# Four unread transposes of the identity on PE at the end of each step of the first batch

## The chip, the cores and the metric

One Trainium2 chip, of which the program uses one core. The metric is the device time of one execution in microseconds (us), lower is better. Five engines work side by side, each on its own list of instructions in the order written: PE (matrix products and transposes), DVE (VectorE), ACT (ScalarE), POOL (GpSimd) and SP, which issues most DMA transfers.

## The reference, cut to what matters

Sliding-window attention with sink keys on 4 batches of 8 heads (768 positions, head size 64), then a gated MLP with a convolution of three taps over the positions:

```
scores = scale * q @ k.T                       # per batch and head
keep   = key < n_sink or 0 <= row - key < window      # n_sink 4, window 128
a      = exp(scores - max) / (sum + 1e-9)      # where keep, else 0
x      = a @ v                                 # heads side by side: 768 x 512 per batch
h      = relu(x @ w_in)                        # 768 x 1024
conv   = conv_w[0]*h[s-1] + conv_w[1]*h[s] + conv_w[2]*h[s+1]
out    = (h * sigmoid(conv)) @ w_out           # 768 x 512 per batch
```

## The kernel before, in words

The heads go in pairs, g = 0 to 15, four pairs to a batch. A pair has six tiles of 128 query rows, t = 0 to 5. One tile of one pair is one step of the loop at line 630. The first batch has 24 steps (NSTB); they run over the first halves of its four pairs and then over the second halves. The other batches run pair by pair.

In step i the loop records, in three slots:

- scores(g, t), line 488: two products on PE, one per head (j = 0, 1), into two PSUM tiles of the tag sc. There are two buffers of this tag, so that j = 0 always has the one and j = 1 the other. Then DVE masks the scores (L508) and reduces them to the row's extreme (L509), ACT takes the exponential with its sum (L512), DVE the reciprocal (L514, L515), POOL the product (L517). In the first batch the products are plain (L339, 260 columns; 128 for t = 0); later each is a sum of two (L342, L343).
- transp of the step before (line 526): two transposes of the probabilities on PE (L532), a copy on ACT (L534), two selections on POOL (L536, L538); at the third tile of a half also the sink columns (L546).
- pv of two steps before (line 558): at the third tile of a half the products with the values (L573, L576) into px, which ACT and DVE store as the MLP's input (L350, L351).

Between the slots stand pieces of other work. The MLP of a part of a batch that is ready is cut into pieces (first products L183, gate L190 to L201, second products L210), spread evenly by a rate over the next steps. For the first batch the first part becomes ready after half of its steps, the second after all of them. The turns of q and k of coming pairs (L318; L276 and L294 from the second batch on) come at due times. In steps 2 to 18 the weights are converted, one piece per step (WHEN, line 35): they are read as 64-bit numbers, narrowed on DVE (L112, L113, L114) and split on ACT and POOL or DVE (L121, L122).

The recorded order isn't the order on the engines. When the program is built, a scheduler puts each engine's instructions in an order of its own, from a model of their times, and adds the waits that the tiles need: a PSUM or SBUF tile may only be written anew when its readers are done. So a change of a few instructions can move all that comes after them. For the waits a tile is one thing: whoever writes one part of it also waits for those who read another.

Of the kernel before, what the change touches and what calls it, by code (L numbers as in the profile page):

```python
# [10 lines left out]
F32 = mybir.dt.float32  # L11
# [6 lines left out]
P = 128  # L18
# [6 lines left out]
SW = 2 * P + NS  # L25
# [6 lines left out]
TRAIL = 2  # L32
NGB = TRAIL + 2
LA = 1
WHEN = list(range(2, 19))


# [23 lines left out]
class Moe:  # L61
# [92 lines left out]
    def need(self, n):  # L154

        while self.done < n:
            self.fetch(self.done + 1)
            self.todo[self.done][2](self.raws[self.done])
            self.done += 1
            self.fetch(self.done + LA)  # L160

# [222 lines left out]
def sink_split(c, m, vsr, b):  # L384

    raw, hi, lo = (m.mp.tile([P, 512], d, tag="st", name=f"sink{n}{b}", bufs=3)[0:NS] for d, n in ((F32, "r"), (F32R, "h"), (F32R, "l")))
    c.nc.sync.dma_start(raw.rearrange("s (h d) -> s h d", d=D), c.v[b].rearrange("h s d -> s h d")[0:NS])
    c.nc.scalar.copy(hi, raw)
    c.nc.vector.tensor_tensor(out=lo, in0=raw, in1=f(hi), op=ALU.subtract)
    for u in range(3):  # L390
        for part, val in enumerate((hi, hi, lo)):
            for j in range(2):
                r = SR * part + 2 * NS * u + NS * j
                dst, src = (f(x).rearrange("s (g j d) -> s g j d", j=2, d=D)[:, :, j] for x in (vsr[r:r + NS, u], val))
                c.nc.sync.dma_start(dst, src)


def banded(c):

    nc = c.nc  # L400
    m = Moe(c)
    A = Attn(c, m.x, KW, m.mp, m.ps)
# [4 lines left out]
    ap, ps = A.ap, A.ps  # L407
# [37 lines left out]
    def clear():  # L445
        w = vsr.shape[1] * vsr.shape[2] // 2
        for h in range(2):
            nc.sync.dma_start(f(vsr).rearrange("p u n -> p (u n)")[:, w * h:w * h + w], A.zeros[0:3 * SR, 0:w])
# [29 lines left out]
    def fetch(upto=len(queue)):  # L478

        while free[0] and asked[0] < min(len(queue), upto):  # L480
            free[0] -= 1
            g, nm, half = queue[asked[0]]
            st[g].raw[nm, half] = load_half(c, g, nm, half, c.raw[asked[0] % RAWB])
            asked[0] += 1
# [3 lines left out]
    def scores(g, t):  # L488
        s = st[g]
        lo = 0 if t == 0 else (t - 1) * KW  # L490
        mk = m0 if t == 0 else (m1 if t == 1 else m2)
        cols = slice(NS if t == 0 else 0, KW)
        sm = sms[A.tiles % len(sms)]
        A.tiles += 1
        hf, u = divmod(t, 3)
        if u == 0:
            s.pe[hf] = ap.tile([P, 3, 2, KW], F32, tag="pe", name=f"pe{g}_{hf}")
            if t == 0:
                nc.gpsimd.memset(s.pe[hf][:, 0, :, 0:NS], 0.0)
        pe = s.pe[hf][:, u]  # L500
        pcs = [ps.tile([P, SW], F32, tag="sc", name=f"sc{g}_{t}_{j}", bufs=2) for j in range(2)]
        if t == 0:
            A.scores(s, t, [pc[:, KW:SW] for pc in pcs], lo, lo + P)
        else:
            A.scores(s, t, pcs, lo, lo + SW)
        for j, pc in enumerate(pcs):
            if t:
                nc.vector.copy_predicated(pc[:, KW:SW], before.bitcast(I32), pc[:, 0:P])  # L508
            nc.vector.tensor_tensor_reduce(out=pe[:, j, cols], in0=pc[:, P:SW][:, cols], in1=mk, op0=ALU.add, op1=ALU.min,  # L509
                                           scale=1.0, scalar=3.0e38, accum_out=sm[:, j:j + 1])  # L510
        for j in range(2):
            nc.scalar.activation(pe[:, j, cols], pe[:, j, cols], AF.Exp, bias=sm[:, j:j + 1], scale=-1.0,  # L512
                                 accum_out=sm[:, 2 + 2 * j:3 + 2 * j])
        nc.vector.tensor_reduce(out=sm[:, 6:8], in_=sm[:, 2:6].rearrange("p (j e) -> p j e", e=2), op=ALU.add, axis=mybir.AxisListType.X)  # L514
        nc.vector.reciprocal(sm[:, 8:10], sm[:, 6:8])  # L515
        for j in range(2):
            nc.gpsimd.tensor_scalar(pe[:, j, cols], pe[:, j, cols], sm[:, 8 + j:9 + j], 1.0, ALU.mult, ALU.mult)  # L517
# [40 lines left out]
    def pv(g, t):  # L558

        s = st[g]  # L560
        hp = g % NPAIR
        hf, u = divmod(t, 3)
        if u < 2:
            return
        px = ps.tile([P, 3, P], F32, tag="px", name=f"px{g}_{hf}").rearrange("p t k -> p (t k)")
        first = 3 * hf
        tiles = range(first + 2, max(0, first - 1) - 1, -1)
        for kt in tiles:
            pT = s.pT.pop((kt, hf)).rearrange("p h a k -> p h (a k)")
            lo, hi = max(kt, first), min(kt + 1, first + 2)  # L570
            cols = slice(P * (lo - kt), P * (hi - kt) + P)
            for j in range(2):
                nc.tensor.matmul(px[D * j:D * j + D, P * (lo - first):P * (hi - first) + P], s.v[:, kt, j, :], pT[:, j, cols],  # L573
                                 start=(kt == tiles[0]), stop=False, skip_group_check=True)
        for w in range(1 - hf, 3):
            nc.tensor.matmul(px[:, P * w:P * w + P], (vsr if g >= NPAIR else c.vs)[:, w, P * hp:P * hp + P], s.sT, start=False, stop=(w == 2),  # L576
                             skip_group_check=True)
        A.xout(g, hf, px)
# [3 lines left out]
    def prep(n):  # L582

        g, half = jobs[n]
        if g >= NPAIR and half:
            return []
        if g >= PLAIN:
            return A.prep(g, st[g], ahead)
        if half == 0 and g % 2 == 0:
            kks.append(f(ap.tile([P, 4, T, KW], F32R, tag="kk", name=f"kk{g}")))  # L590
        out = []
        for h in (half, half + 1)[0:1 + g // NPAIR]:
            out += A.prep32(g, h, st[g], kks[g // 2][:, g % 2], "po" if g < NPAIR and h == 0 else "h", ahead)
        return out

    def values(n):
        g, half = jobs[n]
        if g < NPAIR:
            st[g].v = load_v(c, g, n % 2, *((2, T) if half else (0, 3)))
        elif half == 0:  # L600
            st[g].v = load_v(c, g, g % 2)

    def coming(n):

        last = 2 * NPAIR - 2
        if n < last:
            return [(n + 1, -0.4, 1.8)]
        if n == last:
            return [(n + 1, -0.4, 1.4), (n + 2, 1.4, 5.6)]
        return [(n + 2, -0.4, 5.1)] if n % 2 == 0 and n + 2 < len(jobs) else []  # L610
# [10 lines left out]
    NSTB = NPAIR * T  # L621
# [8 lines left out]
    for i in range(NST + D2):  # L630
        if i < NST:
            n, g, t = steps[i]
            if t % 3 == 0:
                for n1, lo, hi in coming(n):
                    new = prep(n1)
                    todo += [(i + lo + (hi - lo) * (k + 1) / len(new), x) for k, x in enumerate(new)]
            if g >= NPAIR or t % 3 == 2:
                fetch()
            if t == 0 and g and g % NPAIR == 0:
                after = i + 3 if g > NPAIR else i  # L640
            if i == after:
                sink_split(c, m, vsr, g // NPAIR)
            if n + 1 < len(jobs) and (t % 3 == 2 if n < 2 * NPAIR else t == 3):
                values(n + 1)
        if i == NSTB // 2:
            clear()
        m.need(min(sum(i >= w for w in WHEN), len(m.todo)))
        for slot in range(SLOTS):
            if slot == 0 and i < NST:
                scores(g, t)  # L650
            if slot == 1 and 0 <= i - D1 < NST:
                transp(*steps[i - D1][1:])
            if slot == 2 and 0 <= i - D2 < NST:
                pv(*steps[i - D2][1:])
                if i - D2 + 1 in cuts:
                    while fill:
                        fill.pop(0)()
                    lo, hi, span = cuts[i - D2 + 1]
                    fill = m.pieces(lo, hi)
                    rate = len(fill) / (span - 0.5)  # L660
                    acc = 0.0
            acc += rate / SLOTS
            while acc >= 1.0 and fill:
                fill.pop(0)()
                acc -= 1.0
            while todo and i + (slot + 1) / SLOTS >= todo[0][0]:
                todo.pop(0)[1]()
    while fill:
        fill.pop(0)()

# [70 lines left out]
def attention_gated_mlp(ctx: ExitStack, tc: tile.TileContext, q, k, v, n_sink, window, w_in, conv_w, w_out, out):  # L741
# [33 lines left out]
    with tc.If(fast == 1) as cmp:  # L775
        with ExitStack() as es:
            c.es = es
            banded(c)
# [32 lines left out]
```

## Time and profile before

| what | us |
|---|---|
| median of three runs | 489.8 |
| lowest and highest of them | 489.42, 490.3 |
| the profiled execution's own time | 490.03 |
| its span, from the first to the last instruction | 488.3 |
| PE busy | 457.4 (94% of the span) |
| DVE busy | 348.4 (71%) |
| ACT busy | 340.5 (70%) |
| POOL busy | 312.7 (64%) |
| mean granted clock of PE | 0.983 of full speed |

The span begins with the first instruction on the core; 1.73 us of the profiled execution's own time lie outside of it. A busy time holds an instruction from its start to its end. PE's matrix instructions overlap, so that a busy PE isn't one at its peak. The trace shows a product of 32-bit numbers as two instructions and a transpose of 128 columns as one. The granted clock is the share of full speed that PE was given in a stretch.

### The profile page before, as it was taken

Reading aid. Unit: us, or ns where it says so; the run is one execution under the profiler, and the core shown is the slowest. Engines: PE = TensorE matmul, PEld = TensorE weight load, DVE = VectorE, ACT = ScalarE, POOL = GpSimd, SP = SyncE. Lnnn points to the kernel's source line nnn. Section 1 sums busy time; section 2 is a strip of 40 time slices with the busy share of each in tenths; the row PEclk is TensorE's granted clock in tenths of the full one; section 3 lists DMA queues with packets and bytes.
Section 4 is the critical chain, followed back from the end, with each engine's and each line's share of the span. In section 5 each row is a group of like instructions: output and inputs, shape, how many; then the busy total and the mean of one; then the engine's idle time right before and its main releaser. Section 6 shows DMA issues by size and latency. Waiting matters only on the chain.

```text
span 488.3 us, 10470 instructions
## 1 busy us (share of the span) xinstructions
PE 457.4 (94%) x3149; PEld 389.7 (80%) x3149; DVE 348.4 (71%) x1212; ACT 340.5 (70%) x1086; POOL 312.7 (64%) x614
## 2 busy tenths in 40 slices
PE   2887798899999999999999999999999999999995
PEld 2555477688889888888888888888888888999993
DVE  4798989957968777786677585886675665656553
ACT  3887858778878977786877786876776754545451
POOL 3584796867976867684758577685764564344441
PEclk9988989999999999999999999999999999999998
DMA  5778653537234132334132332324021100101011
GB/s 147 211 229 212 172 168 79 126 85 188 67 72 116 61 83 66 87 96 99 60 77 58 85 81 60 70 63 98 24 55 33 44 3 0 44 2 44 1 44 53
DMA packets 87307, 41.03 MB, mean 84 GB/s; under 512 B 80160, under 2 KB 80184, under 8 KB 87240
## 3 DMA queue, kind: packets, MB, share of 16 engines
q1 hardware_dynamic: 87096, 39.99, 31.5%
q8 instruction: 28, 0.46, 0.4%
q14 instruction: 39, 0.32, 0.2%
q10 hardware_dynamic: 144, 0.26, 0.2%
HBM read 27.60 MB, written 6.29 MB: 69 GB/s over the span
## 4 chain that ended last, share of the span: by engine, by line
PE 80%; DVE 7%; DMA 3%; issue 3%; ACT 2%; POOL 2%; SPq 1%; DVEq 0%; ACTq 0%; POOLq 0%
PE po L210 27%; PE ph L183 26%; PE px L573 8%; PE sc L342 4%; PE pts L532 4%; PE sc L343 3%; PE px L576 2%; PE tq L276 2%; PE tk L294 2%; PE sc L339 2%; POOL pe L517 1%; DVE sc L508 1%; DMA wi_1r<-in_moe_w_in_dram 1%; DVE pe L509 1%; DVE stm L113 1%
## 5 line engine op out<-in xcount | busy, mean ns | idle before, releaser
L210 PE MATMUL po<-woH,g 128*128 128x512 f32 x384 | 142.0, 409 | 1.2 <-POOL g L200 1.0
L183 PE MATMUL ph<-xH,wiH 128*128 128x258 f32 (+1 forms) x384 | 112.2, 292 | 1.2 <-ACT X L255 1.2
L183 PE MATMUL ph<-xH,wiL 128*128 128x258 f32 (+1 forms) x384 | 109.0, 284 | 0.0
L183 PE MATMUL ph<-xL,wiH 128*128 128x258 f32 (+1 forms) x384 | 108.8, 284 | 0.0
L517 POOL TENSOR_SCALAR pe<-pe,sm 128x132 f32<-128x132 f32 (+1 forms) x192 | 82.8, 442 | 34.9 <-DVE sm L515 27.2
L512 ACT ACTIVATE pe<-pe,sm 128x132 f32<-128x132 f32 (+1 forms) x192 | 77.5, 406 | 15.8 <-DVE sm L509 14.7
L200 POOL TENSOR_SCALAR g<-t 128x256 fp32r<-128x256 f32 x96 | 42.2, 439 | 70.7 <-DVE t L198 50.8
L195 DVE SCALAR_TENSOR_TENSOR t<-hb,cw,t 128x256 f32<-128x256 f32 x96 | 54.0, 562 | 36.6 <-ACT t L194 36.1
L201 POOL TENSOR_TENSOR g<-t,g 128x256 fp32r<-128x256 f32 x96 | 75.2, 784 | 5.6
L210 PEld LDWEIGHTS po<-woH,g 128*128 128x128 f32 x384 | 68.7, 189 | 11.6 <-POOL g L200 2.6
L183 PEld LDWEIGHTS ph<-xH,wiH 128*128 128x128 f32 x384 | 73.0, 190 | 5.5 <-ACT X L255 1.6
L210 PE MATMUL po<-woL,g 128*128 128x512 f32 x192 | 76.4, 398 | 0.0
L183 PEld LDWEIGHTS ph<-xH,wiL 128*128 128x128 f32 x384 | 72.9, 190 | 2.1
L183 PEld LDWEIGHTS ph<-xL,wiH 128*128 128x128 f32 x384 | 72.8, 190 | 0.7
L197 ACT ACTIVATE t<-t 128x256 f32<-128x256 f32 x96 | 40.1, 418 | 33.8 <-DVE t L196 33.4
L198 DVE SCALAR_TENSOR_TENSOR t<-t,hb 128x256 f32<-128x256 f32 x96 | 47.5, 494 | 20.1 <-ACT t L197 19.0
L508 DVE COPY_PREDICATED sc<-before,sc 128x128 f32<-128x128 int32 x160 | 45.6, 291 | 22.6 <-PE sc L343 19.1
L509 DVE CUSTOM_DVE_ANT_0 pe<-sc,m 128x132 f32<-128x132 f32 (+1 forms) x192 | 54.0, 288 | 10.3 <-PE sc L343 7.8
L190 ACT ACTIVATE hb<-ph 128x258 f32<-128x258 f32 (+1 forms) x96 | 37.0, 386 | 31.4 <-PE ph L183 30.7
L536 POOL TENSOR_SCALAR_AFFINE_SELECT pT<-pT 128x256 f32<-128x256 f32 x80 | 38.2, 477 | 31.4 <-ACT pT L534 31.1
L196 DVE SCALAR_TENSOR_TENSOR t<-hb,cw,t 128x256 f32<-128x256 f32 x96 | 54.1, 564 | 4.1
L194 ACT ACTIVATE t<-hb,cw 128x256 f32<-128x256 f32 x96 | 49.2, 513 | 7.7 <-POOL g L201 3.9
(124 smaller groups left out, 930.2 us busy)
## 6 DMA issues: line engine op xcount, KB each, us to landing
raw<-in_q_dram SPq DMA_DIRECT2D x64, 96.0 KB
raw<-in_k_dram SPq DMA_DIRECT2D x64, 96.0 KB
out_dram<-stm SPq DMA_DIRECT2D x23, 256.0 KB
kk<-kk SPq DMA_DIRECT2D x24, 198.0 KB
vraw<-in_v_dram SPq DMA_DIRECT2D x24, 192.0 KB
wi_0r<-in_moe_w_in_dram SPq DMA_DIRECT2D x2, 512.0 KB
wi_1r<-in_moe_w_in_dram SPq DMA_DIRECT2D x2, 512.0 KB
wi_2r<-in_moe_w_in_dram SPq DMA_DIRECT2D x2, 512.0 KB
```

The lines of the kernel that those rows point to most:

```text
L183: nc.tensor.matmul(u.h[:, 0:W], w[:, cc, ff * P:(ff + 1) * P], x[:, cc, t0:t1], start=(i == 0), stop=(i == len(prods) - 1))
L194: nc.scalar.mul(a, prev, cw[:, 0, ff:ff + 1])
L195: nc.vector.scalar_tensor_tensor(out=e, in0=this, scalar=cw[:, 1, ff:ff + 1], in1=a, op0=ALU.mult, op1=ALU.add)
L196: nc.vector.scalar_tensor_tensor(out=a, in0=nxt, scalar=cw[:, 2, ff:ff + 1], in1=e, op0=ALU.mult, op1=ALU.add)
L198: nc.vector.scalar_tensor_tensor(out=a, in0=e, scalar=1.0, in1=this, op0=ALU.add, op1=ALU.mult)
L200: nc.gpsimd.tensor_scalar(u.g[:, 0], a, 1.0, 1.0, ALU.mult, ALU.mult)
L201: nc.gpsimd.tensor_tensor(out=u.g[:, 1], in0=a, in1=f(u.g[:, 0]), op=ALU.subtract)
L210: nc.tensor.matmul(po[:, 0:c.DM], u.g[:, a, tt * P:(tt + 1) * P], w[:, ff, :], start=(ff == 0 and i == 0), stop=(ff == NFF - 1 and i == 2))
L508: nc.vector.copy_predicated(pc[:, KW:SW], before.bitcast(I32), pc[:, 0:P])
L509: nc.vector.tensor_tensor_reduce(out=pe[:, j, cols], in0=pc[:, P:SW][:, cols], in1=mk, op0=ALU.add, op1=ALU.min, scale=1.0, scalar=3.0e38, ...
L512: nc.scalar.activation(pe[:, j, cols], pe[:, j, cols], AF.Exp, bias=sm[:, j:j + 1], scale=-1.0, accum_out=sm[:, 2 + 2 * j:3 + 2 * j])
L517: nc.gpsimd.tensor_scalar(pe[:, j, cols], pe[:, j, cols], sm[:, 8 + j:9 + j], 1.0, ALU.mult, ALU.mult)
```

## The change

The two score tiles of a step are now whole PSUM banks of 512 columns, of which the scores use the first 260, as before. Columns 384 to 511 of the second one (j = 1) are kept as A.spare. At the end of each of the first 24 steps PE makes four transposes of the 128 x 128 identity into them. Nobody reads what they write. Nothing else is changed: the count of buffers, the work of the other engines and the DMA transfers are the same.

```
+IDLE = 4
...
-        pcs = [ps.tile([P, SW], F32, tag="sc", name=f"sc{g}_{t}_{j}", bufs=2) for j in range(2)]
+        pcs = [ps.tile([P, 512], F32, tag="sc", name=f"sc{g}_{t}_{j}", bufs=2) for j in range(2)]
+        A.spare = pcs[1][:, 384:384 + P]
+        pcs = [pc[:, 0:SW] for pc in pcs]
...
             while todo and i + (slot + 1) / SLOTS >= todo[0][0]:
                 todo.pop(0)[1]()
+        if i < NSTB:
+            for k in range(IDLE):
+                nc.tensor.transpose(A.spare, c.ident, c.ident)
```

The scheduler gives all engines a new order. The 96 transposes stand in 24 groups, most of them whole. Three places on PE show what happens. In the names below, sc_3_0 is the tile of step t = 3 and j = 0, ph and po are the MLP's first and second products, trq and trk turns of q and k, pts the transposed probabilities; what an instruction waits for stands in brackets by engine (Activation is ACT, DMAHW a transfer). Lines of the kernel after are 1 to 6 higher than before: L339 is now L340, L532 is L535, and the new transposes are L673.

The first place is PE at the second and third product pair of the kernel. Before:

```order
L318 MATMUL trq_220<-ident,raw_69 128x128 x2
L339 MATMUL sc_1_0_227<-kk_174,X_179 128x260 [waits DVE_49,Activation_49]
L339 MATMUL sc_1_1_228<-kk_174,X_179 128x260 [waits DVE_49]
L318 MATMUL trk_245<-ident,raw_70 128x128 [waits DMAHW4_49,DMAHW3_49,PE_49]
L318 MATMUL trk_245<-ident,raw_70 128x128 x2
L532 MATMUL pts<-ident,pe_0_206 128x128 [waits Pool_49]
L339 MATMUL sc_2_0_265<-kk_174,X_179 128x260 [waits DVE_49,PE_49]
```

The same place on PE after:

```order
L340 MATMUL sc_1_0_231<-kk_174,X_179 128x260 [waits DVE_49,Activation_49]
L673 MATMUL sc_0_1_209<-ident 128x128 [waits DVE_49]
L673 MATMUL sc_0_1_209<-ident 128x128 x3
L319 MATMUL trk_249<-ident,raw_70 128x128 [waits DMAHW4_49,DMAHW3_49,PE_49]
L319 MATMUL trk_249<-ident,raw_70 128x128 x2
L535 MATMUL pts<-ident,pe_0_206 128x128 [waits Pool_49]
L340 MATMUL sc_1_1_232<-kk_174,X_179 128x260 [waits DVE_49,PE_49]
L340 MATMUL sc_2_0_273<-kk_174,X_179 128x260 [waits PE_49]
```

The group of the first step waits for DVE, which reads the same tile; the second product of the second step, sc_1_1, now comes behind the group, a turn and a transpose.

The second place is PE in the second half of the first batch, about 55 us into the span before, where the first MLP pieces begin. Before:

```order
L532 MATMUL pts<-ident,pe_1_670 128x128 [waits Pool_49]
L339 MATMUL sc_3_0_827<-kk_174,X_701 128x260 [waits DVE_49,PE_49]
L339 MATMUL sc_3_1_828<-kk_174,X_701 128x260 [waits DVE_49,PE_49]
L339 MATMUL sc_4_0_894<-kk_174,X_701 128x260 [waits DVE_49,PE_49]
L339 MATMUL sc_4_1_895<-kk_174,X_701 128x260 [waits DVE_49,PE_49]
L339 MATMUL sc_5_0_973<-kk_174,X_701 128x260 [waits DVE_49,PE_49]
L532 MATMUL pts<-ident,pe_1_670 128x128 [waits Activation_49,Pool_49]
L532 MATMUL pts<-ident,pe_1_670 128x128 [waits Pool_49]
L210 MATMUL po_948<-woH,g_808 128x512 [waits Pool_49]
```

The same place on PE after:

```order
L184 MATMUL ph_867<-xL_117,wiH 128x258
L673 MATMUL sc_5_1_829<-ident 128x128 [waits DVE_49]
L673 MATMUL sc_5_1_829<-ident 128x128 x3
L340 MATMUL sc_3_1_888<-kk_174,X_749 128x260 [waits DVE_49,PE_49]
L340 MATMUL sc_4_0_958<-kk_174,X_749 128x260 [waits PE_49]
L535 MATMUL pts<-ident,pe_1_718 128x128 [waits Activation_49,Pool_49]
L535 MATMUL pts<-ident,pe_1_718 128x128 [waits Pool_49]
L673 MATMUL sc_3_1_888<-ident 128x128 [waits DVE_49]
L673 MATMUL sc_3_1_888<-ident 128x128 x3
L340 MATMUL sc_4_1_959<-kk_174,X_749 128x260 [waits DVE_49,PE_49]
L549 MATMUL tk_5_911<-ident,sk_1_912 96x128 [waits Activation_49]
L184 MATMUL ph_932<-xH_116,wiH 128x258
```

Where five products with scores stood in a row, each behind a wait for DVE, they now stand apart, with the groups, two transposes and an MLP unit among them.

The third place is PE at the first scores of the second batch, about 100 us into the span before. Before (tq is a turn of q in the second batch):

```order
L532 MATMUL pts<-ident,pe_1_1192 128x128 [waits Pool_49] x2
L276 MATMUL tq_1272<-identr,nq_1241 128x128 [waits Activation_49]
L276 MATMUL tq_1272<-identr,nq_1241 128x128 x2
L342 MATMUL sc_0_0_1398<-kk_1156,X_1244 128x128 [waits DMAHW1_49,DVE_49,PE_49]
L343 MATMUL sc_0_0_1398<-kk_1156,X_1244 128x128
L210 MATMUL po_948<-woH,g_1235 128x512 [waits Pool_49]
```

The same place on PE after:

```order
L673 MATMUL sc_4_1_1342<-ident 128x128 [waits DVE_49]
L673 MATMUL sc_4_1_1342<-ident 128x128 x3
L340 MATMUL sc_5_1_1429<-kk_297,X_1135 128x260 [waits DVE_49,PE_49]
L277 MATMUL tq_1454<-identr,nq_1405 128x128 [waits Activation_49]
L277 MATMUL tq_1454<-identr,nq_1405 128x128 x2
L535 MATMUL pts<-ident,pe_1_1276 128x128 [waits Pool_49] x2
L343 MATMUL sc_0_0_1494<-kk_1236,X_1328 128x128 [waits DMAHW4_49,PE_49]
```

The last but one of the groups stands right ahead of the first batch's last score product, which in turn is close to the second batch's first; the last group comes 18 rows behind the latter.

## The prediction

> **What bounds the kernel now.** I read the page first, its span and the slices of PE and of PE's clock.
>
> ```profile
> span 488.3 us, 10470 instructions
> PE   2887798899999999999999999999999999999995
> PEclk9988989999999999999999999999999999999998
> ```
>
> A slice is 12.2 us. From the ninth on (98 us) PE is full at full clock, to the end. Before that it has gaps, and the clock is lower in places. So the end is PE's work plus what it loses in the first 100 us, which is also where the change puts its transposes. I cut these 100 us by a table of busy times (per row: stretch, its length, PE, PEld, DVE, ACT, POOL, each with its count, then PE's clock).
>
> ```profile
> 7.66:28.14 20.48, 16.37 (x83) 11.78 (x82) 16.46 (x79) 17.20 (x60) 11.97 (x28) 1.00 0.83 221
> 28.14:41.79 13.65, 9.32 (x51) 6.15 (x49) 12.86 (x46) 11.62 (x39) 12.42 (x23) 0.87 0.75 214
> 41.79:48.61 6.82, 6.74 (x40) 5.24 (x41) 5.03 (x14) 3.99 (x11) 1.36 (x4) 0.75 0.87 240
> 48.61:65.68 17.07, 12.91 (x66) 9.38 (x65) 16.64 (x56) 12.99 (x43) 13.98 (x20) 0.80 0.55 156
> 65.68:69.09 3.41, 3.41 (x22) 2.99 (x22) 1.62 (x5) 2.45 (x8) 3.41 (x5) 1.00 0.46 154
> 69.09:96.40 27.31, 23.37 (x154) 18.10 (x153) 26.54 (x78) 20.64 (x61) 20.77 (x32) 1.00 0.53 128
> 96.40:106.64 10.24, 10.24 (x78) 8.83 (x79) 5.22 (x23) 7.66 (x29) 7.79 (x19) 1.00 0.20 45
> ```
>
> The reader sees stages with different limits. From 28.14 to 41.79, 48.61 to 65.68 and 69.09 to 96.40 us DVE is busy 94%, 97% and 97% of the time, and PE has 4.33, 4.16 and 3.94 us of gaps: there DVE sets the pace. From 41.79 to 48.61 PE is full, at a clock of 0.75, and DVE has gaps. From 96.40 on PE is full at full clock and DVE half idle: there each added PE instruction is paid for. In the first stretch nobody is full; it is a chain over all engines.
>
> Then the clock. It changes only on a grid of 3.41 us (the same table, PE alone, cut at that grid).
>
> ```profile
> 14.49:17.90 3.41, 2.25 (x14) 1.00 0.64 146
> 28.14:31.55 3.41, 1.63 (x10) 1.00 0.92 258
> 31.55:34.96 3.41, 3.33 (x11) 0.50 0.85 276
> 38.38:41.79 3.41, 0.93 (x7) 1.00 1.11 265
> 41.79:45.20 3.41, 3.33 (x16) 0.50 0.98 261
> 55.44:58.85 3.41, 1.47 (x6) 1.00 0.60 190
> 58.85:62.27 3.42, 1.84 (x4) 0.50 0.00 1
> 62.27:65.68 3.41, 3.41 (x13) 0.50 0.53 154
> 72.51:75.92 3.41, 1.82 (x14) 1.00 0.97 236
> ```
>
> Three windows in which PE was busy 1.63, 0.93 and 1.47 us are followed by one at half clock; those with 1.82 and 2.25 us are not. The line runs between 1.63 and 1.82 us of 3.41. Four windows ran at half clock.
>
> **The change part by part.** The wider PSUM tile costs nothing: the products write the same 260 columns, the count of buffers is the same, and no other engine gets an instruction. What is added is 96 transposes. Their price is the spacing in a row of like instructions, at full clock and at half:
>
> ```profile
> 92.72 0.27 PE L532 MATMUL pts<-ident,pe 128*128 128x128 f32 x1
> 78.18 0.49 PE L318 MATMUL trq<-ident,raw 128*128 128x128 f32 x3
> 14.36 0.33 PE L532 MATMUL pts<-ident,pe 128*128 128x128 f32 x1
> 13.72 0.85 PE L318 MATMUL trk<-ident,raw 128*128 128x128 f32 x3
> ```
>
> Three take 0.49 us where one takes 0.27: (0.49 - 0.27) / 2 = 0.11 us each; at half clock (0.85 - 0.33) / 2 = 0.26. A group of four takes 0.44 us of PE, 24 groups 10.6 us. This is the upper bound of the price, all on the path; the lower one is nothing, less what the clock gives back. Where the groups fall follows from the scores (line 339, PE alone; a step has four such instructions).
>
> ```profile
> 7.66:28.14 20.48, 10.57 (x36) 1.00 0.83 221
> 28.14:41.79 13.65, 4.56 (x14) 0.87 0.75 214
> 69.09:96.40 27.31, 6.11 (x21) 1.00 0.53 128
> 96.40:106.64 10.24, 0.96 (x4) 1.00 0.20 45
> ```
>
> That is 9 steps before 28.14, 3.5 to 41.79, about 5 from 69.09 to 96.40 and the last one behind it; the remaining 6 lie from 41.79 to 69.09. The order after spreads them more evenly.
>
> The groups also bring a wait. Each waits until DVE has read the second score tile of its step, because the tile counts as one thing. On PE the next step's second product stood behind the same release already, so the release isn't new. New is what is queued behind the group besides it: in the order after a turn of k and a transpose (the first place), and 0.44 us between DVE's release and the next score. DVE is covered as long as it has other work, the other head's scores and the weights. PE did wait for DVE before, and the reverse was small in the DVE-bound stages (PE's waits over the first 110 us; DVE's mask from 28 to 97 us).
>
> ```profile
> PE sc L339 <- DVE sm L509: 4.3, 7, 1.7
> L508 DVE COPY_PREDICATED sc<-before,sc 128x128 f32<-128x128 int32 x29 | 8.2, 286 | 1.1 <-PE sc L339 0.9
> ```
>
> Now the sum, stage by stage.
>
> To 28.14 us: 9 groups, 4.0 us, against 4.1 us of gaps in a chain in which PE feeds DVE and ACT. Between 0 and 4.0; I take 0.9, nearer to the bottom, since these gaps are as long as the groups together.
>
> 28.14 to 69.09 us: about 9 groups, 4.0 us, against 8.5 us of gaps in the two DVE-bound stretches. I take 0. The cover is the weights' narrowing on DVE; if it were gone, it would cost up to 4.0.
>
> 69.09 to 96.40 us: 5 to 6 groups, 2.4 us, against 3.9 us of gaps, but PE is 86% busy and DVE 97%, so a delay on either has little room. Between 0 and 2.4; I take 1.2, half.
>
> Behind 96.40 us: PE is full, and what falls there costs 0.44 us a group. In the order after, two groups stand about the second batch's first score (the third place), which before comes at 100.01 us: 0.9 us.
>
> ```profile
> 100.01 0.29 PE L342 MATMUL sc<-kk,X 128*128 128x128 f32 x1
> ```
>
> The clock gives something back. A group adds 0.44 to 0.60 us of busy PE to a window (0.60 with the last one's own 0.27). 1.63 and 1.47 would become over 2.0, above the line; 0.93 would become about 1.5, below it. So the half clock at 31.55 and at 58.85 goes, and that at 41.79 stays unless two groups fall into its window. The first is worth nothing, for DVE sets the pace there. The second made the full window from 62.27 to 65.68 do work worth half its time, 1.7 us; yet what DVE missed behind it was POOL's work on a weight:
>
> ```profile
> 68.59 0.61 DVE L112 TENSOR_SCALAR stm<-stm 128x512 int32<-128x512 int32 x1 [1.79 <-POOL wiL L122]
> ```
>
> So of these 1.7 us I count 1.0. The sum: 0.9 + 0 + 1.2 + 0.9 - 1.0 = +2.0 us. With the profiled execution's own 490.03 us (0.05% above the median of the runs, 489.8) this gives 492.0 us. Its own range takes 0.44 per group for two more and for five more groups on the path, and the clock's full 1.7: 490.0 to 494.5.
>
> A rule speaks against the clock's share. The row first: from 14.49 to 17.90 us PE was busy 2.25 us, most of it transposes (lines 318 and 532 alone, same table):
>
> ```profile
> 14.49:17.90 3.41, 1.11 (x7) 1.00 0.64 146
> 14.49:17.90 3.41, 0.47 (x2) 1.00 0.64 146
> ```
>
> Without them 0.67 us remain, less than the 1.47 us of products after which the clock halved, and yet it stayed at 1.00. So transposes count here. The Trainium skill, "TensorE: Matmul & The Clock Gate", section "Part 4: PE-mode transpose", says that the clock doesn't come up for work in transpose mode, since the monitor doesn't take it for a busy PE in the same way. By that rule nothing is given back, and the sum would be +3.0 instead of +2.0; this trace speaks against it with one window.
>
> **The rivals.**
>
> The clock pays (faster). The groups keep all windows above the line, and lie in PE's stalls. Place: the values' product at 41.87 us at half clock, on the chain of the first MLP input, against the same at full clock.
>
> ```profile
> 41.87 2.40 PE L573 MATMUL px<-pT,vraw 128*64 128x128 f32 x12 [1.73 <-POOL pT L538]
> 44.21 1.17 PE L576 MATMUL px<-sT,roomH 96*128 96x128 f32 x4
> 50.16 1.30 PE L573 MATMUL px<-pT,vraw 128*64 128x128 f32 x12 [0.64 <-POOL pT L538]
> 51.39 0.71 PE L576 MATMUL px<-sT,roomH 96*128 96x128 f32 x4
> ```
>
> (2.40 - 1.30) + (1.17 - 0.71) = 1.6 us, and 1.7 us from the window at 62.27: 3.3 less, 0.9 more behind 96.40: 487.6 us. For it: four windows at half clock, and an order that spreads the scores where PE now stands idle in a row:
>
> ```profile
> 57.90 0.68 PE L339 MATMUL sc<-kk,X 128*128 128x260 f32 x2 [1.67 <-DVE sm L509]
> 59.71 1.21 PE L339 MATMUL sc<-kk,X 128*128 128x260 f32 x2 [1.13 <-DVE sm L515]
> 61.63 1.21 PE L339 MATMUL sc<-kk,X 128*128 128x260 f32 x2 [0.71 <-DVE sm L509]
> ```
>
> Against it: the window before 41.79 needs 0.8 us more, and DVE is at 97% anyway.
>
> The wait decides (slower). Each group delays the next score, and DVE runs dry. Place: the steps up to 28.14 and from 69.09 on, 14 groups by 0.44 = 6.2, and 0.9 behind: +7.1, 497.1 us. It decides once DVE waits for the second score tile by over 0.2 us a step (24 steps: 4.8 us, where the row above shows 0.9). Against it: on DVE the releasing step is mostly followed by the other head's mask (0.29 us in the row of line 508) and a weight's narrowing (0.61 us in the row of line 112).
>
> Transposes don't count for the clock: +3.0, 493.0 us.
>
> All groups lie in gaps, and the clock doesn't matter, since DVE sets the pace: 490.0 us. For it: the gaps up to 96.40 are larger than 10.6 us in sum. Against it: PE and DVE must then fit each other better than now.
>
> **How the numbers follow.** About 0.2%, 1 us, can be told from no change. The forecast gets 0.38 (0.30 of it slower, 0.08 within 1 us), the clock that pays 0.30, transposes that don't count 0.10, the wait 0.09, all hidden 0.13. Faster 0.30, same 0.08 + 0.13 = 0.21, slower 0.30 + 0.10 + 0.09 = 0.49. The range goes from a little below the clock's 487.6 to just short of the wait's 497.1: 487.2 to 496.5.
>
> **What would show it.** Right: 96 transposes in the profile after, 0.11 us apart; half clock in at most two windows behind 20 us; DVE's busy share from 69 to 96 us a little lower; PE full from about 99 us. Wrong towards faster: a clock at 1.00 throughout and the second batch's first scores (line 342, now 343) before 100.0 us in the profile. Wrong towards slower: DVE waits of several us for line 340's products, or half clock as before.

## The result and the profile after

The kernel after takes 497.67 us (median of 4 runs, 495.56 to 498.44), the one before on the same chip 489.91 us (4 runs, 489.42 to 490.3): ratio 1.0154, 95% interval 1.0129 to 1.018. It is slower by 7.8 us, outside of the range that was given. The profiled execution took 498.44 us, the longest of the four. Some executions of oa_tiny, ob_tiny, hb_late2 and of the kernel before, in the experiments below, were slow ones; all medians are of the others.

The page after: its span, PE's slices and clock.

```profile
span 496.7 us, 10671 instructions
PE   3888889899999999999999999999999999999995
PEclk9999989989999999999999999999999999999999
```

Read alone, this looks like a gain: PE is fuller in the first 70 us, and the clock is higher (mean 0.992, before 0.983). A slice is 12.4 us, and PE is full from the ninth on. So the loss can't be seen in these digits; it is in what PE was full of.

Five of the same stretches as before, of all engines (stretch, its length, then PE, PEld, DVE, ACT, POOL with their counts, PE's clock).

```profile
7.66:28.14 20.48, 15.82 (x93) 12.46 (x93) 15.88 (x70) 16.96 (x56) 11.11 (x26) 1.00 0.83 221
28.14:41.79 13.65, 11.53 (x75) 7.45 (x71) 11.38 (x45) 9.95 (x33) 10.75 (x18) 1.00 0.76 238
48.61:65.68 17.07, 13.61 (x87) 10.21 (x88) 15.36 (x52) 14.03 (x41) 15.24 (x20) 0.99 0.68 202
69.09:96.40 27.31, 26.20 (x179) 21.75 (x177) 19.65 (x63) 18.23 (x54) 19.51 (x33) 1.00 0.34 78
96.40:106.64 10.24, 8.72 (x42) 6.57 (x43) 5.45 (x21) 5.40 (x19) 4.77 (x10) 0.83 0.47 109
```

Compare DVE's column with that of before. In the three stretches in which DVE set the pace it was busy 12.86, 16.64 and 26.54 us; now 11.38, 15.36 and 19.65. From 69.09 to 96.40 us DVE fell from 97% to 72%, while PE rose from 23.37 to 26.20 us. By the view of waits DVE stood there for 6.6 us behind ACT and for only 0.6 us behind PE's scores; ACT itself stood 2.4 us behind transfers of the second batch's q, for which it didn't wait before, and 2.0 us behind PE. SP issued the first of these transfers at 84.82 us, before at 78.70. And from 96.40 to 106.64 us, where PE had been full at full clock, it now has gaps and a clock of 0.83.

What PE waited for, and what one group on DVE (the mask) waited for. The first line was not there before; before, PE's chief waits in the first batch's loop were for DVE (4.3 us), and DVE's mask waited 2.0 us for line 339's products over the whole span.

```profile
PE pts L535 <- POOL pe L520: 5.3, 8, 1.6
PE sc L340 <- DVE sm L512: 1.6, 3, 0.6
...
DVE sc L511 <- PE sc L340: 5.2, 4, 4.0
```

One of DVE's waits is 4.04 us long. Its place, and PE's rows up to it:

```profile
105.45 0.30 DVE L511 COPY_PREDICATED sc<-before,sc 128x128 f32<-128x128 int32 x1 [4.04 <-PE sc L340]
```

```profile
99.66 0.45 PE L549 MATMUL tk<-ident,sk 128*96 128x128 f32 x1 [0.79 <-ACT sk L548]
99.76 0.77 PE L211 MATMUL po<-woH,g 128*128 128x512 f32 x1
...
101.61 1.05 PE L673 MATMUL sc<-ident 128*128 128x128 f32 x4
102.31 0.93 PE L211 MATMUL po<-woH,g 128*128 128x512 f32 x2
103.08 0.37 PE L277 MATMUL tq<-identr,nq 128*128 128x128 f32 x3
103.29 0.35 PE L184 MATMUL ph<-xH,wiH 128*128 128x258 f32 x1
...
104.81 1.04 PE L340 MATMUL sc<-kk,X 128*128 128x260 f32 x4
...
111.26 0.30 PE L343 MATMUL sc<-kk,X 128*128 128x128 f32 x1
```

While DVE waits, PE works off MLP products (L211, L184), one group at half clock (1.05 us) and a turn of q; the scores that DVE waits for (L340) stand behind them. The second batch's first score comes at 111.26 us; before it came at 100.01.

**A way to measure it.** Since PE is full behind some 120 us in both kernels, what counts is how much of PE's own work is done by a given time. I gave each matrix instruction, the new transposes left out, the mean distance to the next one that its form has behind 150 us, where PE is full (0.242 us for an MLP product of 512 columns, 0.124 for one of 258, 0.144 for a score product of 260), and added up. The table, worked out so from the trace of each kernel's profiled execution, says by how many us of work a kernel is behind the kernel before at 40, 70, 100, 110 us and at 480; the kernels are those of the next section.

```
                                           40     70    100    110    480
after                                      1.9    3.8    3.7    7.1    8.6
oa_none    new order, no transposes        2.5    4.2    4.1    7.5    8.2
ob_full    old order, all groups           1.9    1.5    3.0    3.2    2.8
ob_first12 old order, steps 0 to 11        2.0    2.4    1.8    1.8    1.3
ob_last12  old order, steps 12 to 23       0.0    2.0    2.0    2.2    1.9
ca_none    new order to 99 us, then old    1.9    2.2    2.1    3.2    2.8
cb_none    old order to 98 us, then new    0.0    2.5    1.8    3.0    4.6
```

After loses 3.8 us up to 70 us and another 3.4 from 100 to 110. The first number is less sure than it looks, because each row is one execution, and executions of the same order differ. Up to 70 us cb_none has the order of the kernel before on every engine and is 2.5 us behind it all the same; ca_none has the order of oa_none there, and is 2.2 us behind where oa_none is 4.2. Between 20 and 70 us oa_none's execution ran four windows at half clock, ca_none's two. What an order costs is therefore taken from the medians.

### The profile page after: what moved, and what is told of

Its sections match the earlier page's. It is cut to its first block, busy times and chain, and to the rows that moved or that the text cites. A ratio compares the mean times of both kernels' runs of the same rounds, so it can differ in the third digit from the quotient of the medians.

```text
span 496.7 us, 10671 instructions
## 1 busy us (share of the span) xinstructions
PE 468.9 (94%) x3245; PEld 397.9 (80%) x3245; DVE 347.0 (70%) x1212; ACT 340.9 (69%) x1086; POOL 313.9 (63%) x614
## 4 chain that ended last, share of the span: by engine, by line
PE 80%; POOL 6%; DVE 4%; DMA 3%; ACT 2%; SPq 2%; issue 2%; POOLq 0%; DVEq 0%; ACTq 0%
PE ph L184 27%; PE po L211 26%; PE px L576 8%; PE pts L535 4%; PE sc L343 4%; PE sc L344 3%; POOL pe L520 2%; PE tq L277 2%; PE px L579 2%; DMA raw<-in_q_dram 1%; PE tk L295 1%; SPq L360 1%; POOL wiL L123 1%; POOL pT L539 1%; DVE stm L115 1%
## 5 line engine op out<-in xcount | busy, mean ns | idle before, releaser
L211 PE MATMUL po<-woH,g 128*128 128x512 f32 x384 | 142.7, 412 | 0.0
L184 PE MATMUL ph<-xH,wiH 128*128 128x258 f32 (+1 forms) x384 | 112.3, 292 | 0.0
L184 PE MATMUL ph<-xH,wiL 128*128 128x258 f32 (+1 forms) x384 | 109.7, 286 | 0.0
L184 PE MATMUL ph<-xL,wiH 128*128 128x258 f32 (+1 forms) x384 | 109.1, 285 | 0.0
L520 POOL TENSOR_SCALAR pe<-pe,sm 128x132 f32<-128x132 f32 (+1 forms) x192 | 84.2, 450 | 33.1 <-DVE sm L518 24.3
L211 PEld LDWEIGHTS po<-woH,g 128*128 128x128 f32 x384 | 69.2, 190 | 11.4 <-POOL g L201 1.5
L202 POOL TENSOR_TENSOR g<-t,g 128x256 fp32r<-128x256 f32 x96 | 74.0, 771 | 5.5
L211 PE MATMUL po<-woL,g 128*128 128x512 f32 x192 | 76.5, 398 | 0.0
L184 PEld LDWEIGHTS ph<-xH,wiH 128*128 128x128 f32 x384 | 73.1, 190 | 3.8 <-issue 0.6
L184 PEld LDWEIGHTS ph<-xH,wiL 128*128 128x128 f32 x384 | 73.2, 191 | 2.1
L184 PEld LDWEIGHTS ph<-xL,wiH 128*128 128x128 f32 x384 | 73.1, 190 | 0.8
L199 DVE SCALAR_TENSOR_TENSOR t<-t,hb 128x256 f32<-128x256 f32 x96 | 49.5, 516 | 21.4 <-ACT t L198 20.3
```

The lines of the kernel that those rows point to most:

```text
L184: nc.tensor.matmul(u.h[:, 0:W], w[:, cc, ff * P:(ff + 1) * P], x[:, cc, t0:t1], start=(i == 0), stop=(i == len(prods) - 1))
L199: nc.vector.scalar_tensor_tensor(out=a, in0=e, scalar=1.0, in1=this, op0=ALU.add, op1=ALU.mult)
L202: nc.gpsimd.tensor_tensor(out=u.g[:, 1], in0=a, in1=f(u.g[:, 0]), op=ALU.subtract)
L211: nc.tensor.matmul(po[:, 0:c.DM], u.g[:, a, tt * P:(tt + 1) * P], w[:, ff, :], start=(ff == 0 and i == 0), stop=(ff == NFF - 1 and i == 2))
```

## The experiments

My theory when I began: the transposes cost about what I had summed, +2, and the rest comes from the new order of all the other instructions. The rivals: the groups' wait for DVE (the rival of the prediction whose 497.1 us lies nearest), or the transposes' time on PE.

**Order and transposes apart.** Kernel and order can be had separately: the program is built twice, once with and once without the groups. The second build gets a tie between each two neighbours of an engine's list of the first one, which orders them and makes nobody wait. In the traces PE, DVE, ACT, POOL and SP of oa_none run in the order of the kernel after, and those of ob_full in the order of the kernel before, the groups left out. The old order tied without groups wasn't run; ob_first12 below has the ties and half of the groups and is 0.45 us above the kernel before, so the ties by themselves cost little.

```
+def follow(c, here, order):
+    last = {}
+    for key, engine in order:
+        if key in here:
+            if engine in last:
+                c.tc.add_manual_dep(here[key], last[engine], info, reason="order")
+            last[engine] = here[key].name
...
-                nc.tensor.transpose(A.spare, c.ident, c.ident)
+                one = nc.tensor.matmul(A.spare[:, 0:4], c.ident, c.ident[:, 0:4], start=True, stop=True)
```

oa_none has the order of the kernel after and no groups; ob_full has the order of the kernel before, with the 24 groups where the scheduler finds room for them. In oa_tiny and ob_tiny a product of four columns stands for each transpose (the last two lines of the diff), so that the wait stays and the time on PE should go.

> The order of every engine as the changed kernel has it, without the 96 transposes. If their time on PE is what costs (work): back to about 490.5 us, within 1.5 of the kernel before. If the scheduler's new order is what costs (order): 496 to 498 us, as changed. If the groups' waits for DVE cost (wait): 490 to 491 us, for the waits go with them.

> The order of the kernel before on every engine, with the 24 groups of four transposes put among it on PE where the scheduler finds them due. Work: 495 to 499 us, the 10.6 us of transposes less what gaps take. Order: 489 to 492 us. Wait: 493 to 498 us.

> The order of the changed kernel, with each transpose replaced by a product of 4 columns that has the same place and the same waits, so that 96 instructions stay and nearly all of their 10.6 us go. Work: 490 to 492 us. Order: 496 to 498 us. Wait: 496 to 498 us, since the waits stay.

> The order of the kernel before, with 96 products of 4 columns in the groups' places, with their waits. Work: 489.5 to 491.5 us. Order: 489 to 491 us. Wait: 493 to 497 us.

Measured, beside 490.08 us for the kernel before on the same chip:

| kernel | median us | ratio, 95% interval |
|---|---|---|
| oa_none | 496.13 | 1.0133, 1.0098 to 1.0168 |
| ob_full | 492.54 | 1.005, 1.0033 to 1.0066 |
| oa_tiny | 501.47 | 1.0235, 1.0208 to 1.0262 |
| ob_tiny | 502.99 | 1.029, 1.0257 to 1.0323 |

The new order alone, with the same instructions as before and nothing added, costs 6.0 us. All 24 groups in the old order cost 2.5. So the groups' time and their wait together are worth 2.5 us, and the rival of the wait, with its 7.1, is refuted as the price of the groups by themselves. That the groups cost anything on top of the new order isn't resolved: the intervals of oa_none (+4.8 to +8.2) and of the kernel after (+6.3 to +8.8) overlap.

PE's clock and waits in oa_none, and its first score of the second batch:

```profile
PEclk9978899989999999999999999999999999999998
```

```profile
PE pts L537 <- POOL pe L522: 6.4, 8, 2.1
...
PE sc L342 <- DVE sm L514: 2.3, 3, 1.3
```

```profile
111.34 0.30 PE L345 MATMUL sc<-kk,X 128*128 128x128 f32 x1
```

The same wait for POOL as in the kernel after, and the same place of the first score, with no transpose added. In ob_full the clock is as high as in the kernel after (0.994), and the first score comes at 103.14:

```profile
PEclk9999989999999999999999999999999999999998
```

```profile
103.14 0.29 PE L345 MATMUL sc<-kk,X 128*128 128x128 f32 x1
```

The pair with four columns failed as a control: it costs 10.5 us more than the transposes that it was to make cheaper (ob_tiny against ob_full; 3.8 in the new order, oa_tiny against the kernel after). The group of ob_tiny:

```profile
L678 PEld LDWEIGHTS sc<-ident x192: 186/192/337, 12.5 to 112.9; 128*128 128x128 f32 x192
L678 PE MATMUL sc<-ident x192: 168/253/355, 12.9 to 112.9; 128*128 128x4 f32 x192
```

Each product is two instructions, each with a weight load of its own: 192 instructions of 0.25 us instead of 96 transposes of 0.27, and 192 weight loads of 0.19 us instead of 96 of 0.14. A product of four columns is not a short one. Nothing about the wait follows from these two kernels.

**Fewer groups, or elsewhere, with the scheduler free.** Here nothing is tied, so each kernel gets an order of its own.

```
-IDLE = 4
+IDLE = 1                                  (e3_one)
-        if i < NSTB:
+        if i < NSTB // 2:                 (e5_first12)
+        if NSTB // 2 <= i < NSTB:         (e6_last12)
```

In e7_behind the four transposes are recorded right behind the step's scores, not at the end of the step.

> One transpose in a group instead of four, the scheduler free. On PE, 3.5 score products stand ahead of a step's turned probabilities on average, against 4.2 before and 3.1 in the changed kernel. If the loss is the lookahead that groups at the end of a step take from the scores: about 493 to 495 us. If any new order costs about 6 us by chance: 495 to 498. If it were PE's time after all: 490.5 us, a quarter of 2.5 more than before.

> Groups in steps 0 to 11 alone. Lookahead in these 3.3 (4.75 before), in the others 3.2 (3.6 before). Lookahead: 493 to 496 us, if early steps count as much as late ones; near 491 if DVE has enough else to do there and only the late steps count. Chance order: 495 to 498. PE's time: 491 to 492.

> Groups in steps 12 to 23 alone. Lookahead 4.75 in the first twelve steps as before, 2.8 in the others (3.6 before). Lookahead: 492 to 494 us if all steps count alike; 495 to 497, nearly all of the loss, if only the late steps count. Chance order: 495 to 498. PE's time: 491 to 492.

> The same four transposes per step, but right behind the step's scores instead of at its end, so that they don't hold the next step's second score product back to the end of the step; the scheduler free. The lookahead is 4.1, as before. Lookahead: 491.5 to 493.5 us, only the 2.5 us that the groups cost in the old order. Chance order: 495 to 498 us. PE's time: 492.5 us.

| kernel | median us (before 490.10) | ratio, 95% interval |
|---|---|---|
| e3_one | 491.58 | 1.0038, 1.0023 to 1.0054 |
| e5_first12 | 491.08 | 1.0026, 1.0009 to 1.0042 |
| e6_last12 | 497.68 | 1.0143, 1.0117 to 1.017 |
| e7_behind | 495.75 | 1.0113, 1.0091 to 1.0136 |

Half of the groups cost 1.0 us in the first twelve steps, and 7.6 in the last twelve, as much as all of them. I held then that it hangs on how many score products PE has ahead of a step's transposes of probabilities (4.2 products before, 3.1 after on average). That fell with e7_behind, where it is 4.1, near to before, and the kernel loses 5.7 us.

**The same halves in the old order, and each half of the new order alone.** ob_first12 and ob_last12 have the groups of e5 and e6, but the old order on all engines. ca_none and cb_none have no groups; they change from the one order to the other at PE's 310th instruction. That isn't at 75 us, as I thought when I wrote what I expected: a 32-bit product is one instruction in the program and two in the trace. By the traces cb_none leaves the old order behind row 411 of PE, at 98 us (97 in the kernel before), and ca_none the new one behind row 409, at 99 us (103 in the kernel after). So the change-over lies at about 100 us, and nothing here divides the loss at 70 us.

```
+    head = first[:pe[310]]
+    seen = {key for key, engine in head}
+    FOLLOW[0] = head + [y for y in second if y[0] not in seen]
```

> The old kernel's order, transposes in the first twelve steps only. By the account of TensorE's time in the run with all of them in the old order, they take nothing up to 70 us (clock given back 0.6 us more than they cost): 489.5. By the prediction's terms for that stretch, +0.9 less 1.0: 490. If all groups cost alike, half of +2.5: 491.3.

> The old kernel's order, transposes in steps 12 to 23 only. By the same account they hide little behind 70 us: +3 to +3.4, 493. By the prediction's terms for that stretch, 1.2 + 0.9: 492.2. If all groups cost alike, 491.3.

> No transposes; every engine follows the new kernel's order up to TensorE's 310th instruction (about 75 us), and the old kernel's order from there. If the new order costs all along (work done on TensorE by 70 us was 4.2 us behind the kernel before in the run with the whole new order), about +4, 494; if all its cost of some 6 us arises behind 70 us, where the two rows of value products part, 490; if an early loss is caught up later because TensorE has idle time to spare until 115 us, 490 to 491.

> No transposes; the old kernel's order up to TensorE's 310th instruction, the new kernel's order from there. If the new order costs all along, +2 to +3.5, 492 to 493.5; if the cost lies wholly behind 70 us, the whole +6, 496; if it needs both halves, 490.

| kernel | median us (before 490.08) | ratio, 95% interval |
|---|---|---|
| ob_first12 | 490.53 | 1.0009, 1.0001 to 1.0018 |
| ob_last12 | 491.23 | 1.0031, 1.0018 to 1.0044 |
| ca_none | 495.20 | 1.0116, 1.0095 to 1.0137 |
| cb_none | 494.01 | 1.0074, 1.0058 to 1.009 |

In the old order the halves cost 0.45 and 1.15 us (0.0 to 0.9 and 0.9 to 2.2), 1.6 together; the 2.5 of all (1.6 to 3.2) agrees with that within the intervals. The groups of e6_last12, which cost 7.6 us with a free scheduler, cost 1.15 when the old order is kept: the rest is order. And each half of the new order costs by itself, 5.1 and 3.9 us. That is more than the 6.0 of the whole, so the two don't simply add: a part of what the first half loses the second would have lost anyway, or the change-over itself costs something. Neither side of it has the loss alone.

Ahead of the change-over the two kernels show what each order leaves in PE's waits, from 20 to 70 us. First ca_none, with the new order, then cb_none, with the old one:

```profile
PE pts L537 <- POOL pe L522: 5.7, 7, 2.1
```

```profile
PE px L578 <- POOL pT L543: 3.8, 3, 3.0
PE sc L342 <- DVE sm L514: 3.8, 5, 1.7
```

cb_none waits as before does, for DVE and for the values' operand; ca_none as the kernel after does, for POOL's scaled probabilities.

Next DVE from 85 to 110 us, on both sides of the change-over, in three kernels: before, after, oa_none (stretch, length, DVE's busy time and count).

```profile
85.00:100.00 15.00, 12.69 (x51) 1.00 0.47 110
100.00:110.00 10.00, 6.56 (x26) 1.00 0.45 103
```

```profile
85.00:100.00 15.00, 8.38 (x29) 0.98 0.40 89
100.00:110.00 10.00, 3.72 (x17) 0.86 0.34 79
```

```profile
85.00:100.00 15.00, 7.96 (x28) 1.00 0.39 87
100.00:110.00 10.00, 4.08 (x20) 0.83 0.36 84
```

With and without transposes the new order leaves DVE 12.1 and 12.0 us of work in 25 us, where it had 19.25 before. cb_none, which takes the new order only at 98 us, has 13.13 us up to 100 and 3.75 behind; ob_full, in the old order, has 14.02 and 4.96. PE did more of the MLP early: from 70 to 96 us its MLP products took 14.6 us (14.0 in oa_none, 10.8 before), and from 96 to 100 us 0.2 us (0.4 in oa_none, 2.9 before). There it ran short of work (2.03 us busy from 95.96 to 99.37 us after, a row below), and its clock halved, in oa_none too.

**One move of the order alone.** Of the new order's first part I suspected one thing: PE's transposes of probabilities (L537 here) stand too early, so that PE waits for POOL with score products queued behind. Four kernels without groups move only these, among PE's first 310 instructions (640 in ha_late2all), past up to two neighbouring score or MLP products.

```
+    for i in turn:
+        if i < 310 and kind.get(pe[i][0]) == "P":
+            for k in range(2):
+                if kind.get(pe[i + step][0], "-") in "SM":
+                    pe[i], pe[i + step] = pe[i + step], pe[i]
+                    i += step
...
```

ha_late2 takes the new order and moves them later, ha_late2all does so over 640 instructions, hb_early2 takes the old order and moves them earlier, hb_late2 later.

> No transposes of the identity; the new kernel's order, but among TensorE's first 310 instructions each transpose of probabilities stands up to two products (scores or MLP) later. In the run of the whole new order TensorE waited 6.4 us for GpSimd's scaled probabilities with score products queued behind. If that place of the probabilities' transposes is what the new order costs in its first part, those waits go and the time falls by 3 to 4, to 492.5; if the order is only late (work is late whatever stands first), 496 as before.

> As the first kernel of this call, but over TensorE's first 640 instructions (to about 140 us). If the place of these transposes is also what the new order costs behind 70 us: 490 to 491. If the second part's cost is another (MLP products done early, none left while the softmax runs): the same as the first kernel, 492.5.

> No transposes of the identity; the old order, but among TensorE's first 310 instructions each transpose of probabilities stands up to two products earlier. If their place decides: waits for GpSimd's scaled probabilities of some 5 us appear, +3 to +5, 493 to 495. If not: 490.

> No transposes of the identity; the old order, with each transpose of probabilities among TensorE's first 310 instructions up to two products later. If fewer waits for GpSimd and VectorE are what counts: 489 or a little under. If the values' products then come late (they need these transposes): 491 to 492.

| kernel | median us (before 490.83) | ratio, 95% interval |
|---|---|---|
| ha_late2 | 499.65 | 1.017, 1.0145 to 1.0196 |
| ha_late2all | 499.46 | 1.0195, 1.0168 to 1.0223 |
| hb_early2 | 495.64 | 1.011, 1.0089 to 1.0132 |
| hb_late2 | 493.15 | 1.0042, 1.0027 to 1.0058 |

Earlier costs 4.8 us in the old order, as expected. But later costs too, 2.3 us in the old order, and in the new one it doesn't give the loss back: 499.65, not 492.5. PE's waits say what happens. ha_late2, hb_early2, hb_late2, each over the whole span:

```profile
PE sc L342 <- DVE sm L514: 9.7, 10, 2.7
...
PE pts L537 <- POOL pe L522: 3.3, 4, 1.7
```

```profile
PE pts L537 <- ACT pT L539: 6.5, 4, 2.1
PE pts L537 <- POOL pe L522: 3.8, 4, 2.7
PE sc L342 <- DVE sm L514: 2.8, 4, 1.8
```

```profile
PE sc L342 <- DVE sm L514: 7.1, 9, 1.7
```

Moved later, the wait for POOL falls from 6.4 to 3.3 us, and the wait for DVE grows from 2.3 to 9.7: the scores, now first, stand in front of a tile that DVE hasn't read yet. Moved earlier, the waits for POOL and ACT appear, the longer ones for ACT, which I had not expected. The old order stands between the two. A part of what ha_late2 loses is clock: its profiled execution has seven windows at half clock, the kernel before four. So this one place on PE isn't the cause. The waits read as a balance that any move upsets, but that is argued from these moves alone; every change of the order alone that I tried costs between 2.3 us (hb_late2) and 8.8 (ha_late2) of 490. None of the sixteen kernels is faster than before.

What stays open: what part of the second half's loss (3.4 us from 100 to 110 in after, 3.4 in oa_none) is the half clock there (a window of 3.41 us at half speed, 1.7 us), and what the short pieces and the waits around it. Nor is it tested how much of it comes from the later transfers of q: ACT waits 2.4 us for them in after and 2.0 in oa_none, from 69 to 96 us. I didn't take that apart. Shown is that the order costs the time; which waits in it, stays open.

## Why the prediction was wrong, point by point

- **What bounds the kernel: right.** PE's work plus what PE loses in the first 100 us sets the end. After is 8.6 us of work behind, of which 7.1 up to 110 us.
- **The price and number of the transposes: right.** There are 96 of them (duration in ns: least, median, longest; then the first and last start). PE and its weight load together stood idle ahead of them for DVE for 1.2 us, PE alone for 0.4.

```profile
L673 PE MATMUL sc<-ident x96: 270/273/421, 12.7 to 114.3; 128*128 128x128 f32 x96
...
  DVE sm L512: 1.2, 2
```

  In a window at full clock with one whole group (line 673 alone) the four take 0.60 us, where one takes 0.27: (0.60 - 0.27) / 3 = 0.11 us apart.

```profile
72.06:75.48 3.42, 0.60 (x4) 1.00 0.47 105
```

  The price at half clock, 0.26 us, was read from rows at 13.72 and 14.36 us, where the profile has no record of the clock yet and its column shows 1.00; the sum doesn't use it. The group at half clock in the kernel after gives about the same: (1.05 - 0.33) / 3 = 0.24.

- **The stages' terms: right in sum, in the old order, and partly by luck.** 0.9 + 0 + 1.2 + 0.9 - 1.0 = +2.0 was for all groups; ob_full measured +2.5 (1.6 to 3.2). By halves: the -1.0 was read from windows between 55 and 66 us, where steps from 12 on stand, not in the first twelve, as I wrote before the runs of the halves. So the first twelve steps were to cost 0.9 + 0, and cost 0.45; the rest was to cost 1.2 + 0.9 - 1.0 = 1.1, and cost 1.15. But no run shows the -1.0 by itself, and the window that it was for ran at half clock still (next point). The sum's own range was a little too wide for its terms, which give about 490.4 to 494.2.
- **The clock: right in the count, not in the place.** Half clock in two windows behind 20 us, at most two was forecast; ob_full has one, the kernel before four. But the windows at 31.55 and 58.85 us were to go and that at 41.79 to stay. In ob_full those at 31 and 41 are gone, and the one behind 58 us is there:

```profile
58.45:61.87 3.42, 1.51 (x5) 1.00 0.43 153
61.87:65.28 3.41, 3.29 (x10) 0.50 0.00 0
```

  Transposes count: in the same order ob_full's six executions have mean clocks of 0.990 to 0.999, the eleven of the kernel before on that chip 0.982 to 0.990, so the rule of the Trainium skill ("TensorE: Matmul & The Clock Gate", "Part 4: PE-mode transpose"), by which work in transpose mode isn't counted as a busy PE, doesn't hold here.
- **The failed step: the order.** I read the new order at three places, called it one that "spreads them more evenly", and gave it no term but 0.9 us for two groups at the third. The sum was one for groups put into the old order. The new order of the other 3149 matrix instructions, and of the other engines, costs 6.0 us without any group. This term was missing, with its sign and its bounds, and so the range ended 1.2 us short.
- **The rival of the wait: near in time, wrong in cause.** Its 497.1 us is close to 497.67, and DVE does wait several us for line 340, as it said. But the wait was to come from the groups standing ahead of the scores. It is there in oa_none without groups (5.1 us, one of 3.7):

```profile
DVE sc L513 <- PE sc L342: 5.1, 5, 3.7
```

  In ob_full, with all groups and the old order, DVE waits 6.7 us for these products, 4.7 more than the kernel before. That is above the 4.8 from which I said that the wait decides, and yet the kernel loses 2.5 us and not 7.1. The rows of ob_full and of before:

```profile
DVE sc L513 <- PE sc L342: 6.7, 12, 1.4
```

```profile
DVE sc L508 <- PE sc L339: 2.0, 5, 0.6
```

- **DVE's share from 69 to 96 us: direction right, size not.** "A little lower" was 72% instead of 97%, and that was the sign of the loss. Not the groups had displaced DVE's work, but the new order: oa_none without a group has 76% (20.77 of 27.31 us), ob_full with all groups 91% (24.86).

## What to carry to other kernels

Where a scheduler orders all engines, an edit of a few instructions is two edits: what it adds, and a new order for everything else. Give the new order a term of its own, here between 0.5 us (e5_first12 less ob_first12) and 6.4 (e6_last12 less ob_last12) of 490, and look for a loss first: none of the new orders here was faster than the old one; and take the two apart by building with the old order kept. In the trace, look at what an engine is full of, not at how full it is: PE rose and the clock rose, and the engine that set the pace, DVE, had fallen from 97% to 72% in the stretch from 69 to 96 us.

## What the runs showed of the hardware

A product of 128 x 128 by four columns costs more than a transpose of 128 columns: two instructions of 0.25 us with two weight loads of 0.19 us, where the transpose is one of 0.27 with one load of 0.14, and 10.5 us on the whole for 96 of them in the old order (502.99 against 492.54 us). Why it is as much as that isn't shown.

The line of the clock isn't as sharp in PE's busy time as I took it (between 1.63 and 1.82 us of a window of 3.41). After, then ob_full, PE alone; each first row is followed by the window in the second:

```profile
61.82:65.24 3.42, 1.58 (x8) 1.00 0.52 199
65.24:68.65 3.41, 3.41 (x17) 0.50 0.00 0
...
95.96:99.37 3.41, 2.03 (x9) 1.00 0.48 109
99.37:102.78 3.41, 3.12 (x10) 0.50 0.76 178
```

```profile
41.39:44.80 3.41, 1.77 (x15) 1.00 1.00 262
44.80:48.21 3.41, 3.16 (x25) 1.00 0.99 268
```

2.03 us of nine instructions were followed by half clock, 1.77 us of fifteen were not, and in ob_first12 not even 1.60 us of thirteen. In ob_tiny half clock followed 3.13 us of busy PE (24.27 to 27.68 us), 16 of whose 24 instructions were products of four columns. So busy time, which holds the latency of each instruction, isn't quite what the clock goes by. In the second window above the group of four is 0.60 us of the 1.77.

An estimate comes nearer. Count each instruction not with its busy time but with its spacing: 0.11 us for 128 columns of 32-bit numbers, in transposes as in products, and 0.242 us for 512 columns of the MLP and of the second batch's products. Take the 380 windows of 3.41 us at full clock between 12 and 112 us in sixteen of the profiles (without those with products of four columns, for which no spacing was taken). 39 of them are followed by half clock. A line at 1.42 us so counted has 6 windows on the wrong side, the best line in busy time, at 1.84 us, has 12. With the transposes left out of the count no line has fewer than 28 on the wrong side. That, too, says that transposes count.
